# Delta-rule attention in front of a mixture of experts: chunks of 32 tokens in four partition quadrants instead of 64 in two halves, with the TensorE order written out

## The chip, the core and the metric

The kernel runs on one core of a Trainium2 chip. The metric is the device time of one execution in microseconds (us). A second view is one profiled execution, whose trace gives every instruction's start and duration on five engines: TensorE (PE for matmuls, PEld for the weight loads that precede them), VectorE (DVE), ScalarE (ACT), GpSimd (POOL) and SyncE (SP, which here only issues DMAs).

## What is computed

Two stages. The first is a delta-rule recurrence over 768 tokens for each of 4 batches and 8 heads, with head dimension 48; its result, 3072 rows of 384, is the input of a mixture of 16 experts (4 groups of 4), of which each row uses one.

```python
B, H, S, D = 4, 8, 768, 48
k_n = k / (norm(k) + 1e-6)
state = zeros(B, H, D, D)
for t in range(S):
    y[:, :, t] = q[:, :, t] @ state
    v_old = state^T k_n[t]
    state += beta[t] * outer(k_n[t], v[t] - v_old)
x = y as (3072, 384)                      # rows are tokens, heads side by side
g = argmax(x @ w_group);  e = argmax(x @ w_expert[g])
out = weight(g) * weight(e) * (relu(x @ w1[g, e]) @ w2[g, e])      # 384 -> 1024 -> 384
```

Everything is fp32.

## The kernel before

**Chunks.** A recurrence over single tokens would be 768 serial steps. The kernel works on chunks of `C = 64` tokens instead. Inside a chunk the corrected values are `w = M f`, where `f` are the values less what the state already holds for these keys, and `M` is the inverse of a unit lower triangular 64x64 matrix built from the products of the keys. One unit `u` is a chunk of two batches: its 128 tokens fill the 128 partitions, batch one in partitions 0 to 63, batch two in 64 to 127 (`halves`). There are `NU = 24` units: 12 chunks times `NG = 2` pairs of batches.

**`prepare(u)`** does what needs no state. GpSimd scales keys and values (`kp` L190, `vh` L193). TensorE transposes the keys (`kt_ps` L198), ScalarE copies them to `kqt` (L200). For each parity of the head number (`hh`) the products keys-by-keys and keys-by-queries go to `g_ps` (L209), VectorE masks them into `gq` and `mm` (L213, L218), and three GpSimd operations form the start of the inverse (L222 to L225). Then the inverse is doubled level by level: with `LEVELS = (2, 4, 8, 16, 32)` there are five levels, and at each, for each `hh`, 8 matmuls of 64x64 give `y_ps` (L239), VectorE masks them into `y` (L242), 16 matmuls (8 at the last level) give `m_ps` (L249, L251), and ScalarE copies them to the next `mm` (L261, at the last level `mt`, L256). A level can't begin before the copy of the level below it is there.

**`advance(u)`** carries the state `s_bd`: `a_ps` (L273, keys by state), `f` (L278), `w_ps` (L284), `w` (L287), the state's increment `d_ps` (L292) added by VectorE (L299), and `outputs(u)`: `o_ps` (L308, L314), copied to `x` (L318).

**`route(c)`** takes the finished rows of one chunk of all four batches: transposes (`t_ps`, L350), logits (`l_ps`, L355), a chain of some thirty short VectorE, ScalarE and GpSimd operations that picks group and expert and counts the rows per expert (`r_ps`, L389 and L391), the store of the rows to `x_dram` (four DMAs on SP, L380), and one matmul group that adds the rows' places to a table (`p_ps`, L423).

**Order.** The main loop over 12 chunks calls `advance` on the two units of the chunk and `prepare` on those of the next one; the framework's scheduler then decides the order in which each engine runs the instructions, TensorE included. Tiles come from pools with a fixed number of buffers; an instruction that writes a tile waits until the tile's former user is done.

**The experts.** After the last chunk the table is turned into indices (L444 to L453), and 16 experts run with two tiles of 128 rows each: gather by indirect DMA (L461), transposes (L473), two matmul layers (L481, L488), scatter (L492). The weights of the first two experts are loaded during the attention, the others while the experts run.

A fp32 matmul is two passes in the trace: a weight load and a matmul for each of two passes. So the page counts 3840 matmuls on L239 where the program has 24 x 2 x 5 x 8 = 1920. "Pass" below means one such pair.

Of the kernel before, what the change touches and what calls it, by code (L numbers as in the profile page):

```python
# [15 lines left out]
C = 64  # L16
LEVELS = (2, 4, 8, 16, 32)
XW = 388


def constants(n_tokens, seq, n_experts, n_group, n_pairs):
    """Masks and counters that depend on the shapes alone, by name."""
# [4 lines left out]
    twice = lambda m: np.concatenate([m, m], axis=0)  # L27
# [6 lines left out]
        "upper": twice(np.concatenate([upper, upper], axis=1)),  # L34
        "eye": twice(eye),
        "low0": twice(-below(1).astype(np.float32)),
        "up0": twice(eye - below(1).T),
        "level": twice(np.concatenate([eye - below(s) for s in LEVELS], axis=1)),
# [3 lines left out]
        "desc": np.tile(np.arange(n_group, 0, -1), (128, n_pairs)),  # L42
# [10 lines left out]
def deltanet_then_moe(  # L53
# [17 lines left out]
    NG = B // 2  # L71
    NCH = S // C
    NU = NCH * NG
# [9 lines left out]
    STATIC = -(-N // (NE * 128))  # L83
    halves = [slice(0, 64), slice(64, 128)]

# [27 lines left out]
    with ExitStack() as first:  # L113
# [5 lines left out]

        k_all = ap_.tile([128, NU, H, D], F32, name="k_all")  # L120
        bt = ap_.tile([128, NU, H], F32, name="bt")
        ssq = ap_.tile([128, NU, H], F32, name="ssq")
        rs = ap_.tile([128, NU, H], F32, name="rs")
        sb = ap_.tile([128, NU, H], F32, name="sb")
        s_bd = ap_.tile([128, B, NP, 2, D], F32, name="s_bd")
        NB = 4
# [3 lines left out]
        def load_k(u):  # L130
            nc.scalar.dma_start(out=k_all[:, u].rearrange("p h d -> p (h d)"), in_=k_d[u])

        def load_qv(u):
            v = io.tile([128, H, D], F32, tag="v", name=f"v{u}")
            nc.sync.dma_start(out=v.rearrange("p h d -> p (h d)"), in_=v_d[u])
            kqt = kqt_[u % NB]
            for hh in range(2):
                nc.sync.dma_start(out=kqt[hh * 64:hh * 64 + D, 1].rearrange("p j t -> p (j t)"),
                                  in_=q_d[u, hh])
            return v  # L140
# [4 lines left out]
        for u in range(NG):  # L145
            load_k(u)
        nc.scalar.dma_start(out=bt.rearrange("p u h -> p (u h)"), in_=beta_d)
        nc.sync.dma_start(out=con, in_=const_d)
        vs = {u: load_qv(u) for u in range(NG)}
        for u in range(NG, NU):  # L150
            load_k(u)
# [4 lines left out]
        zrow = ap_.tile([1, XW], F32, name="zrow")  # L156
# [3 lines left out]
        def root(out_, in_, shape_, name):  # L160
            """sqrt of in_, with a Newton step in fp32 behind the table; gives twice the root."""
            r0 = sm.tile(shape_, F32, tag=name + "0", name=name + "0")
            r1 = sm.tile(shape_, F32, tag=name + "1", name=name + "1")
# [6 lines left out]
        root(sb, bt, [128, NU, H], "rb")  # L170
# [12 lines left out]

        norms(0, NG, nc.vector)

        def prepare(u):
            """Everything of a chunk that does not need the state: keys and values scaled, the
            products of keys and queries, the inverse of the unit lower triangular matrix."""
            v, kqt, kp = vs.pop(u), kqt_[u % NB], kp_[u % NB]
            nc.gpsimd.tensor_tensor(kp[:, :, 0:D], k_all[:, u],  # L190
                                    rs[:, u, :, None].to_broadcast([128, H, D]), op=ALU.mult)
            vh = wk.tile([128, H, D], F32, tag="vh", name=f"vh{u}", bufs=4)
            nc.gpsimd.tensor_tensor(vh, v, sb[:, u, :, None].to_broadcast([128, H, D]),  # L193
                                    op=ALU.mult)
            kt_ps = ps.tile([128, NP, 128], F32, tag="g", name=f"kt_ps{u}")
# [5 lines left out]

            gqs, mts = [], []
            for hh in range(2):
                g_ps = ps.tile([128, NP, 2, C], F32, tag="g", name=f"g_ps{u}_{hh}")
                rows = slice(hh * 64, hh * 64 + D)
                for j in range(NP):
                    for b in range(2):
                        t = slice(b * C, (b + 1) * C)
                        nc.tensor.matmul(g_ps[halves[b], j], lhsT=kqt[rows, 0, j, t],  # L209
                                         rhs=kqt[rows, :, j, t], start=True, stop=True,  # L210
                                         skip_group_check=True)
                gq = wk.tile([128, NP, 2, C], F32, tag=f"gq{hh}", name=f"gq{u}_{hh}", bufs=3)
                nc.vector.tensor_tensor(  # L213
                    gq.rearrange("p j a t -> p j (a t)"),
                    g_ps.rearrange("p j a t -> p j (a t)"),
                    cut["upper"][:, None, :].to_broadcast([128, NP, 2 * C]), op=ALU.mult)
                mm = wk.tile([128, 2, NP, C], F32, tag=f"mm{hh}", name=f"mm{u}_{hh}_0", bufs=3)
                nc.vector.tensor_tensor(  # L218
                    mm[:, 0], g_ps[:, :, 0, :],
                    cut["low0"][:, None, :].to_broadcast([128, NP, C]), op=ALU.mult)  # L220
                eye = cut["eye"][:, None, :].to_broadcast([128, NP, C])
                nc.gpsimd.tensor_tensor(mm[:, 0], mm[:, 0], eye, op=ALU.add)  # L222
                at = wk.tile([128, NP, C], F32, tag=f"at{hh}", name=f"at{u}_{hh}")
                nc.gpsimd.tensor_tensor(at, gq[:, :, 0, :], eye, op=ALU.add)  # L224
                nc.gpsimd.tensor_tensor(  # L225
                    mm[:, 1], at, cut["up0"][:, None, :].to_broadcast([128, NP, C]),
                    op=ALU.mult)
                gqs.append(gq)
                mts.append((at, mm))

            for n in range(len(LEVELS)):
                last = n == len(LEVELS) - 1
                mask = cut["level"][:, n * C:(n + 1) * C]
                for hh in range(2):
                    at, mm = mts[hh]
                    y_ps = ps.tile([128, NP, C], F32, tag="y", name=f"y_ps{u}_{hh}_{n}")
                    for j in range(NP):
                        for b in halves:
                            nc.tensor.matmul(y_ps[b, j], lhsT=at[b, j], rhs=mm[b, 0, j],  # L239
                                             start=True, stop=True, skip_group_check=True)  # L240
                    y = wk.tile([128, NP, C], F32, tag=f"y{hh}", name=f"y{u}_{hh}_{n}")
                    nc.vector.tensor_tensor(y, y_ps,  # L242
                                            mask[:, None, :].to_broadcast([128, NP, C]),
                                            op=ALU.mult)
                    m_ps = ps.tile([128, 2, NP, C], F32, tag="m", name=f"m_ps{u}_{hh}_{n}")
                    for j in range(NP):
                        for b in halves:
                            if not last:
                                nc.tensor.matmul(m_ps[b, 0, j], lhsT=mm[b, 1, j], rhs=y[b, j],  # L249
                                                 start=True, stop=True, skip_group_check=True)  # L250
                            nc.tensor.matmul(m_ps[b, 1, j], lhsT=y[b, j], rhs=mm[b, 1, j],  # L251
                                             start=True, stop=True, skip_group_check=True)
                    if last:
                        new = wk.tile([128, NP, C], F32, tag=f"mt{hh}", name=f"mt{u}_{hh}",
                                      bufs=3)
                        nc.scalar.activation(new, m_ps[:, 1], ACT.Copy)  # L256
                        mts[hh] = new
                    else:
                        new = wk.tile([128, 2, NP, C], F32, tag=f"mm{hh}",
                                      name=f"mm{u}_{hh}_{n + 1}", bufs=3)  # L260
                        nc.scalar.activation(new, m_ps, ACT.Copy)  # L261
                        mts[hh] = (at, new)
            return kqt, kp, vh, gqs, mts

        def advance(u, made):
            """The chunk's outputs, and the state behind it."""
            c, g = u // NG, u % NG
            kqt, kp, vh, gqs, mts = made
            if c > 0:
                a_ps = ps.tile([128, H, D], F32, tag="q", name=f"a_ps{u}")  # L270
                for b in range(2):
                    for j in range(NP):
                        nc.tensor.matmul(a_ps[halves[b], 2 * j:2 * j + 2, :],  # L273
                                         lhsT=kqt[:, 0, j, halves[b]],
# [152 lines left out]
        for c in range(NCH):  # L427
            nxt = range((c + 1) * NG, min((c + 2) * NG, NU))
            for u in nxt:
                vs[u] = load_qv(u)  # L430
# [147 lines left out]
```

## Time and profile before

| what | value |
|---|---|
| time, median of 3 runs | 1143.3 us (1142.66 to 1143.77) |
| span of the profiled execution | 1145.2 us |
| PE busy / PEld busy | 1026.7 us (90%) / 863.4 us (75%) |
| DVE / ACT / POOL busy | 316.1 / 226.8 / 245.5 us |
| passes on TensorE | 16298 |
| first matmul of the attention (L198) | 34.8 us into the span |
| end of the last logits of the attention (L355) | 761.4 us |
| first transpose of the experts (L473) | 776.4 us |

The profiled execution has a span of 1145.2 us, 1.9 us above the median of the timed runs. The table's lower half splits it: 34.8 us of loading and norms without a matmul, some 726 us of attention, 15 us of the last routing, and 369 us of experts. A matmul's row in the trace shows its whole way through the array (218 ns for a pass of 64 columns); several are under way at once, so "busy" says that something is under way and not how dense it is. How dense it is, the starts in the timeline tell. "PEclk" is the share of TensorE's clock that was granted.

### The profile page before, as it was taken

How to read it: one execution, taken by the hardware profiler on the slowest of the kernel's cores; microseconds unless marked ns; L12 is line 12 of the kernel's file. 1: busy time of each engine (PE TensorE's matmuls, PEld its weight loads, DVE VectorE, ACT ScalarE, POOL GpSimd, SP SyncE). 2: the span in 40 equal slices, each digit the busy share in tenths (PEclk: the TensorE clock that was granted, in tenths of full speed). 3: DMA queues.
4: the chain of work that ended last, by engine and by line, in shares of the span. 5: the costliest groups of instructions: out<-in, count | busy, mean ns of one | idle time of the engine just before them, and what ended most of it. 6: DMA issues, size and time to landing. Idle time of an engine off the chain costs nothing. (4 is left out here: it accounts for less than half of the span.)

```text
span 1145.2 us, 35577 instructions
## 1 busy us (share of the span) xinstructions
PE 1026.7 (90%) x16298; PEld 863.4 (75%) x16298; DVE 316.1 (28%) x983; ACT 226.8 (20%) x429; POOL 245.5 (21%) x389
## 2 busy tenths in 40 slices
PE   0698999999999999998999999978999999999996
PEld 0587888888888887888888888866776677677674
DVE  4533434242423334242334242330100100110010
ACT  0132322222222222222222222210110011011000
POOL 5613122222222222122122221102211211221110
PEclk9999899999999999999999999988999999999998
DMA  9500100000100001010100000003545555464520
GB/s 297 209 11 10 31 17 23 23 24 17 30 17 21 26 17 30 10 30 17 31 9 17 16 17 2 17 16 107 190 146 191 165 185 173 165 199 141 192 68 11
DMA packets 41545, 83.49 MB, mean 73 GB/s; under 512 B 4377, under 2 KB 30156, under 8 KB 41394
## 3 DMA queue, kind: packets, MB, share of 16 engines
q1 hardware_dynamic: 33698, 65.30, 17.8%
q0 software_dynamic: 4096, 11.08, 2.9%
q10 hardware_dynamic: 3600, 4.82, 1.3%
q8 instruction: 128, 2.10, 0.8%
q14 instruction: 23, 0.19, 0.0%
HBM read 71.70 MB, written 11.06 MB: 72 GB/s over the span
## 5 line engine op out<-in xcount | busy, mean ns | idle before, releaser
L239 PE MATMUL y_ps<-mm,at 64*64 64x64 f32 x3840 | 227.7, 229 | 47.0 <-POOL mm L222 41.5
L251 PE MATMUL m_ps<-mm,y 64*64 64x64 f32 x3840 | 248.5, 228 | 0.2
L239 PEld LDWEIGHTS y_ps<-mm,at 64*64 64x64 f32 x3840 | 183.4, 140 | 69.3 <-POOL mm L222 51.9
L251 PEld LDWEIGHTS m_ps<-mm,y 64*64 64x64 f32 x3840 | 223.2, 143 | 2.4 <-DVE y L242 1.2
L249 PE MATMUL m_ps<-y,mm 64*64 64x64 f32 x3072 | 216.2, 233 | 1.3
L249 PEld LDWEIGHTS m_ps<-y,mm 64*64 64x64 f32 x3072 | 195.3, 142 | 16.0 <-DVE y L242 15.2
L242 DVE TENSOR_TENSOR y<-y_ps,con 128x256 f32<-128x256 f32 x240 | 101.8, 424 | 371.7 <-PE y_ps L239 368.7
L261 ACT ACTIVATE mm<-m_ps 128x512 f32<-128x512 f32 x192 | 114.7, 597 | 385.8 <-PE m_ps L251 385.8
L481 PE MATMUL h_ps<-xt,w 128*128 128x256 f32 x768 | 171.6, 384 | 8.1 <-DVE xt L475 8.1
L481 PEld LDWEIGHTS h_ps<-xt,w 128*128 128x128 f32 x768 | 145.9, 192 | 31.2 <-DVE xt L475 11.7
L488 PE MATMUL y_ps<-w,hid 128*128 128x384 f32 x512 | 167.7, 486 | 0.0
L488 PEld LDWEIGHTS y_ps<-w,hid 128*128 128x128 f32 x512 | 97.3, 190 | 64.4
L491 DVE TENSOR_SCALAR yo<-y_ps,xg 128x384 f32<-128x384 f32 x32 | 19.8, 618 | 321.0 <-PE y_ps L488 316.5
L484 ACT ACTIVATE hid<-h_ps 128x512 f32<-128x512 f32 x64 | 38.2, 597 | 322.3 <-PE h_ps L481 322.3
L492 POOL DMA_INDIRECT out_dram<-yo,idx x32 | 32.4, 1012 | 289.9 <-DVE yo L491 285.8
L190 POOL TENSOR_TENSOR kp<-k_all,rs 128x384 f32<-128x384 f32 x24 | 19.8, 829 | 303.9 <-PE g_ps L209 185.8
L209 PE MATMUL g_ps<-kqt 48*64 48x128 f32 x768 | 58.9, 284 | 0.7 <-ACT kqt L200 0.7
L224 POOL TENSOR_TENSOR at<-gq,con 128x256 f32<-128x256 f32 x48 | 34.9, 726 | 77.4 <-DVE gq L213 77.4
L198 PE MATMUL kt_ps<-con,kp 128*128 128x128 f32 x96 | 17.1, 300 | 36.4 <-POOL kp L190 34.8
L209 PEld LDWEIGHTS g_ps<-kqt 48*64 48x64 f32 x768 | 43.0, 137 | 2.3 <-ACT kqt L200 1.1
L284 PE MATMUL w_ps<-f,mt 64*64 64x48 f32 x704 | 43.0, 241 | 0.2 <-DVE f L278 0.2
L273 PE MATMUL a_ps<-s_bd,kqt 128*64 128x96 f32 x352 | 42.4, 262 | 0.0
(115 smaller groups left out, 922.2 us busy)
## 6 DMA issues: line engine op xcount, KB each, us to landing
w<-in_w_dram SPq DMA_DIRECT2D x32, 1536.0 KB, 6.8
x_dram<-x SPq DMA_DIRECT2D x48, 97.0 KB, 2.2
k_all<-in_k_dram ACTq DMA_DIRECT2D x24, 192.0 KB, 4.7
v<-in_v_dram SPq DMA_DIRECT2D x24, 192.0 KB, 2.5
kqt<-in_q_dram SPq DMA_DIRECT2D x48, 96.0 KB, 2.2
con<-in_const_dram SPq DMA_DIRECT2D x1, 708.5 KB, 5.2
xg<-x_dram,idx POOLq DMA_INDIRECT x32, 3.2
out_dram<-yo,idx POOLq DMA_INDIRECT x32, 3.3
```

Source lines behind the costliest of these rows:

```text
L209: nc.tensor.matmul(g_ps[halves[b], j], lhsT=kqt[rows, 0, j, t], rhs=kqt[rows, :, j, t], start=True, stop=True, skip_group_check=True)
L224: nc.gpsimd.tensor_tensor(at, gq[:, :, 0, :], eye, op=ALU.add)
L239: nc.tensor.matmul(y_ps[b, j], lhsT=at[b, j], rhs=mm[b, 0, j], start=True, stop=True, skip_group_check=True)
L242: nc.vector.tensor_tensor(y, y_ps, mask[:, None, :].to_broadcast([128, NP, C]), op=ALU.mult)
L249: nc.tensor.matmul(m_ps[b, 0, j], lhsT=mm[b, 1, j], rhs=y[b, j], start=True, stop=True, skip_group_check=True)
L251: nc.tensor.matmul(m_ps[b, 1, j], lhsT=y[b, j], rhs=mm[b, 1, j], start=True, stop=True, skip_group_check=True)
L261: nc.scalar.activation(new, m_ps, ACT.Copy)
L273: nc.tensor.matmul(a_ps[halves[b], 2 * j:2 * j + 2, :], lhsT=kqt[:, 0, j, halves[b]], rhs=s_bd[:, 2 * g + b, j], start=True, stop=True, sk ...
L284: nc.tensor.matmul(w_ps[b, h], lhsT=mts[h % 2][b, h // 2], rhs=f[b, h], start=True, stop=True, skip_group_check=True)
L481: nc.tensor.matmul(h_ps[:, k], lhsT=w1[:, j, (f + k) * 128:(f + k + 1) * 128], rhs=xt[:, j], start=(j == 0), stop=(j == DC - 1), skip_grou ...
L484: nc.scalar.activation(hid[:, f:f + 2], h_ps, ACT.Relu)
L488: nc.tensor.matmul(y_ps, lhsT=hid[:, f, i * 128:(i + 1) * 128], rhs=w2[:, f], start=(f == 0), stop=(f == FC - 1))
```

## The change

The chunk shrinks to `C = 32`, and a unit is now the same 32 tokens of all four batches, one batch in each quadrant of 32 partitions (`quads`). There are 24 units again, but they are now 24 serial steps of the state instead of 12 steps of two. The inverse needs four levels instead of five. Its matmuls are 32x32: for each level 32 for `y_ps` and 64 for `m_ps` (32 at the last), each on the quadrant of the array that its batch's partitions give. Both parities of the head number share one tile and one VectorE or ScalarE operation.

`prepare`, `advance`, `logits` (split from `route`) and `route` become generators that hand over after each stage, and a loop of `period`s of four `tick`s steps them: three chunks are in `prepare` at once, the oldest first, `advance` is three periods behind, `logits` four, and `route` runs once for every `RG = 4` chunks. Inside `tc.manual_schedule` TensorE runs in exactly this order; the other engines' order is still the scheduler's. Most PSUM tiles share one pool of four banks (tag `s`); `g_ps` and the two `d_ps` share two tiles of two banks. The rows' store is 16 DMAs of 32 rows for each `route`, where it was 4 of 64 for each chunk.

```diff
-C = 64
-LEVELS = (2, 4, 8, 16, 32)
+C = 32
+LEVELS = (2, 4, 8, 16)
+RG = 4
...
     halves = [slice(0, 64), slice(64, 128)]
+    quads = [slice(b * C, (b + 1) * C) for b in range(B)]
...
+        def prepare(u):
...
+            kt_ps = ps.tile([128, NP, 128], F32, tag="s", name=f"kt_ps{u}", bufs=4)
...
+            yield
+            g_ps = ps.tile([128, 2, 512], F32, tag="g", name=f"g_ps{u}")
...
+            for j in range(NP):
+                for b in range(B):
+                    for hh in range(2):
+                        rows = slice(hh * 64, hh * 64 + D)
+                        nc.tensor.matmul(g_out[quads[b], hh, j], lhsT=kqt[rows, 0, j, quads[b]],
+                                         rhs=kqt[rows, :, j, quads[b]], start=True, stop=True,
...
+            yield
+            yield
+            yield
+            for n in range(len(LEVELS)):
+                last = n == len(LEVELS) - 1
+                y_ps = ps.tile([128, H, C], F32, tag="s", name=f"y_ps{u}_{n}", bufs=4)
+                for h in range(H):
+                    for b in quads:
+                        nc.tensor.matmul(y_ps[b, h], lhsT=at[b, h], rhs=mm[b, 0, h],
+                                         start=True, stop=True, skip_group_check=True)
+                y = wk.tile([128, H, C], F32, tag="y", name=f"y{u}_{n}", bufs=4)
+                nc.vector.tensor_tensor(y, y_ps, wide(cut["level"][:, n * C:(n + 1) * C]),
+                                        op=ALU.mult)
+                yield
+                m_ps = ps.tile([128, 2, H, C], F32, tag="s", name=f"m_ps{u}_{n}", bufs=4)
+                for h in range(H):
+                    if not last:
+                        for b in quads:
+                            nc.tensor.matmul(m_ps[b, 0, h], lhsT=mm[b, 1, h], rhs=y[b, h],
+                                             start=True, stop=True, skip_group_check=True)
+                    for b in quads:
+                        nc.tensor.matmul(m_ps[b, 1, h], lhsT=y[b, h], rhs=mm[b, 1, h],
+                                         start=True, stop=True, skip_group_check=True)
...
+                yield
+
+        def advance(u):
...
+                for j in range(NP):
+                    for b in range(B):
+                        nc.tensor.matmul(a_ps[quads[b], 2 * j:2 * j + 2, :],
+                                         lhsT=kqt[:, 0, j, quads[b]], rhs=s_bd[:, b, j],
...
+            yield
...
+            yield
...
+                        for b in range(B):
+                            hh = (b + odd) % 2
+                            nc.tensor.matmul(d_out[odd][halves[hh], b // 2, j],
+                                             lhsT=kp[quads[b], 2 * j + hh],
...
+            yield
+            yield
...
+        with tc.manual_schedule(engines={mybir.EngineType.PE}):
+            for period in range(NCH + 7):
+                u = period
+                for tick in range(4):
...
+                    if tick == 2:
+                        if u == 0:
+                            norms(2, 6, nc.gpsimd)
+                        if u == 1:
+                            norms(6, NCH, nc.gpsimd)
+                        if u + 1 < NCH:
+                            scale(u + 1)
+                    for v in (u - 2, u - 1, u):
+                        step("prepare", v)
+                    step("advance", u - 3)
+                    if tick % 2:
+                        step("logits", u - 4)
+                    step("route", (u - 5) // RG)
```

Read along the ticks, TensorE's order within one full period is: `y` of level 2 of the oldest chunk and of level 0 of the middle one (levels counted from 0), `kt` of the youngest, `a`; then `m` of those two levels, `g`, `w`, the state's part of `o`, and the transposes `t` of the chunk before; then `y` of levels 3 and 1, `d`, the rest of `o`; then `m` of levels 3 and 1, the logits `l`, and every fourth period the routing's `r` and `p`.

## The prediction, made before the changed kernel ran

> **What bounds the kernel now.** First the stretches of the span, cut at the first matmul, the last logits and the first transpose of the experts. Columns: length, then busy us and instructions of each engine, the granted clock, DMA.
>
> ```profile
> 0.00:34.80 34.80, 0.00 (x0) 0.00 (x0) 16.30 (x35) 1.75 (x3) 22.28 (x41) 1.00 0.93 317
> 34.80:760.50 725.70, 671.90 (x14902) 603.82 (x14902) 258.04 (x843) 186.38 (x360) 158.45 (x279) 0.95 0.08 23
> 760.50:776.40 15.90, 6.05 (x20) 4.45 (x20) 6.88 (x41) 0.46 (x3) 3.88 (x9) 0.57 0.17 41
> 776.40:1145.20 368.80, 348.70 (x1376) 255.11 (x1376) 34.92 (x64) 38.23 (x64) 60.92 (x62) 0.98 0.45 149
> ```
>
> The change touches the first 776 us; 368.8 us of experts stay. In the attention TensorE has something under way 93% of the time, and no other engine is above 36%. It needs 725.7 / 14902 = 48.7 ns a pass. What a pass costs when nothing waits, the timeline shows within one level of the inverse:
>
> ```profile
> 303.18 0.33 PE L249 MATMUL m_ps<-y,mm 64*64 64x64 f32 x4
> 303.29 0.33 PE L251 MATMUL m_ps<-mm,y 64*64 64x64 f32 x4
> 303.41 0.33 PE L249 MATMUL m_ps<-y,mm 64*64 64x64 f32 x4
> 303.52 0.33 PE L251 MATMUL m_ps<-mm,y 64*64 64x64 f32 x4
> 303.64 0.33 PE L249 MATMUL m_ps<-y,mm 64*64 64x64 f32 x4
> ```
>
> Four passes start every 0.117 us, 29.3 ns each. Two batches work in two tiles of the array, so one tile takes 58.6 ns a pass. The other 19 ns of the 48.7 are waits, changes of tile shape, longer matmuls, and a clock of 0.95. The waits for the copies are visible in the waits' view as PEld m_ps L249 behind DVE (15.2 us) and y_ps L239 behind POOL (48.7 us).
>
> Now the price of a change of tile shape, and of a round trip through ScalarE:
>
> ```profile
> 757.47 0.33 PE L308 MATMUL o_ps<-s_bd,kqt 128*64 128x96 f32 x2
> 757.73 1.01 PEld L314 LDWEIGHTS o_ps<-w,gq 64*64 64x64 f32 x32
> 757.73 1.13 PE L314 MATMUL o_ps<-w,gq 64*64 64x48 f32 x32
> 758.80 0.84 PE L355 MATMUL l_ps<-wr,xt 128*128 128x20 f32 x6
> 758.91 0.49 ACT L318 ACTIVATE x<-o_ps 128x384 f32<-128x384 f32 x1 [1.76 <-PE o_ps L314]
> 759.49 0.52 PE L350 MATMUL t_ps<-con,x 128*128 128x128 f32 x3
> ```
>
> From the last pass of one shape to the first of the next it is 0.16 to 0.17 us (757.56 to 757.73; the o burst's last start, 758.80 less 0.16, to 758.80). A pass of 48 columns (32 in 1.13 us, less the last one's 0.22: 29.4 ns) costs what one of 64 does, so the load of 64 weight columns sets it. l_ps, 128 weight columns and 20 moving ones, takes (0.84 - 0.275) / 5 = 113 ns. The round trip: o ends at 758.86, ScalarE's copy ends at 759.40, the transpose that needs it starts at 759.49: 0.6 us.
>
> **The change: passes.** The program now has 24832 passes in the attention instead of 14902, because each inverse is cut finer: 4 x 32 + 3 x 64 + 32 = 352 matmuls, 704 passes a chunk, against 448 for a unit before. All depends on what a 32x32 pass costs, which the trace does not have. By the two load rows (58.6 ns at 64 columns, 113 at 128: 0.85 ns a column and 4 ns fixed) one tile would take 31 ns. Four quadrants at once make that 7.9 ns a pass. The other end is 29.3 ns, if what I see is a rate of issue and not of the tiles. The nearest row for more than two tiles is a place where y and d interleave:
>
> ```profile
> 92.87 0.22 PE L239 MATMUL y_ps<-mm,at 64*64 64x64 f32 x1
> 92.87 0.26 PE L292 MATMUL d_ps<-w,kp 64*64 64x48 f32 x3
> 92.93 0.22 PE L239 MATMUL y_ps<-mm,at 64*64 64x64 f32 x1
> 92.97 0.23 PE L292 MATMUL d_ps<-w,kp 64*64 64x48 f32 x2
> 92.99 0.22 PE L239 MATMUL y_ps<-mm,at 64*64 64x64 f32 x1
> 93.03 0.23 PE L292 MATMUL d_ps<-w,kp 64*64 64x48 f32 x2
> ```
>
> Ten passes start in 0.16 us, some 17 ns each: 29 ns is no rate of issue, at least in a short burst. A second bound is the fetch of instructions:
>
> ```profile
> q8 instruction: 128, 2.10, 0.8%
> ```
>
> 128 packets took 0.8% of 16 engines x 1145 us, 1.15 us each; they brought 2 x 16298 instructions, 255 a packet, so one packet serves 128 passes: 9.0 ns a pass if the packets follow each other without a gap. I take 9.0, the tile's 7.9 raised to the fetch.
>
> [...]
>
> **One full period**, in us of TensorE:
> - y, m: 704 x 9.0 = 6.3; g: 64 x 9.0 = 0.6
> - w and o: 128 passes of 48 moving columns. L488 of the experts moves 384 columns in 323 ns, 0.84 ns a column, so 44 ns a tile, 11 with four: 1.4
> - a and the state's part of o: 64 passes of 96 columns. Before, one batch after the other, a_ps takes 94 ns a pass ((0.92 - 0.26) / 7 at 301.81); the new loop alternates four tiles, 23.5: 1.5
> - d: 64 passes that load 64 columns, four row tiles, 58.6 / 4 = 14.7: 0.9
> - 7 transposes at 0.124 (kt at 328.39: (0.66 - 0.29) / 3): 0.9; logits 6 x 0.113 = 0.7; p and r, a quarter of 8 x 0.32 + 4 x 0.12: 0.8
> - 12 changes of shape (y-kt-a-m-g-w-o-t-y-d-o-l-y) at 0.17: 2.0
>
> Sum 15.1. **Waits.** The order puts other bursts between each burst and its copy: after y2, y0, kt and a (2.4 us) cover DVE's 0.42 us and the way; m's copies (ACT, 0.60 for 128x512) are covered by g, w, o, t; the state additions (four of 64x384; 0.36 at 64x192, 0.55 at 128x384, taken 0.55: 2.2 us) by o, m3, m1, l, y, kt, 5 us. If that cover is gone, each place costs 0.6 or more. One place has none: in the pool of four banks m3's tile is the one that o leaves, so m3 waits for x (L318): 0.6 us. Queues: DVE gets 5.8 us a period from its rows (0.69 + 0.42 + 4 x 0.42 + 0.55 + 2.2 + 0.2) and 2 of routing, ACT 4.3, POOL 3.9 and 1, all below 15. In each fourth period some 30 routing operations of 0.16 to 0.21 us stand in DVE's order between y's masks, and one of them waits for POOL; m waits behind that. I take 3 us, 0.75 a period; bounds 0 and 8 (all of them in the way). Period: 15.1 + 0.6 + 0.75 = 16.5 us.
>
> **The ends.** The first matmul stays at 34.8: its chain (24 loads on ACT's queue before the root) is the same. POOL then has 13 operations of 0.82 us before the first inverse's start where it had five, so y0 comes at 48 instead of 43; two unfilled periods, bound by round trips, 9 to 10 us each: the first full period begins at 67. 21 full periods follow (chunks 3 to 23 in `prepare`), then four that empty: 14.5, 12, 6, 2.2 = 35 us. The last routing took 15 us up to the experts' first transpose; now 16 stores of the rows stand on SP instead of 4 (0.58 us each in L380's rows, 9.3 us) and the gather waits for all: +4. In full flow SP's stores delay the loads of later queries, which have a whole period. Experts 368.8.
>
> Sum: 67 + 21 x 16.5 + 35 + 19 + 369 = 836 us against a span of 1145.2. The median of the runs is 1.9 us below that span; I leave it out.
>
> **Rivals.**
> 1. Slower: passes start at a fixed rate whatever their size, 29 ns, and the 17 ns was only a filled queue. For: no burst of one line before runs below 26 ns a pass. Against: starts come in pairs 4 ns apart and then nothing for 54, the picture of two busy tiles. Price: y, m, g 768 x 20 ns, w and o 128 x 18, d 64 x 15, a 64 x 6: +19 us, a period of 35.5, 1236 us. It decides from (1145 - 490) / 21 = 31.2 us a period, about 25 ns a pass.
> 2. Two quadrants at a time, or instructions fetched with gaps: 16 ns a pass, +6 us a period, 965.
> 3. The written order covers less than I think: a round trip bare in each tick with its queue, 4 x 1 us: 920.
> 4. The clock. It falls to 0.5 for 3.4 us after gaps; if passes this small count as idle, every matmul doubles: 31 us a period, about 1150, no change.
>
> That the change does nothing is excluded: order and number of passes differ in the build.
>
> **Chances.** Forecast (785 to 900) 58%; 2 and 3 (900 to 1040) 27%; 1 is 8%, 4 is 4%, both at 1100 and above; below 785 (DVE-free, 7.9 ns) 3%. Range 785 to 1040. Runs of one kernel here lie within 0.1%, so 0.2% is what can be told from no change: faster 0.88, same 0.02, slower 0.10.
>
> **What would show it.** In a new m burst, 16 passes in 0.14 us; if 0.26, rival 2; if 0.47, rival 1. From the first transpose of one chunk to that of the next 16.5 us, with no PE gap above 0.7 us but before m3 and in routing periods. PEclk at 1.0 throughout. q8's packets back to back would show the fetch at its limit. I am wrong if TensorE's passes are dense and yet the period is above 20.

## The result: 1161.3 us, 1.5% slower

| kernel | time, median | ratio to the kernel before | mean clock |
|---|---|---|---|
| before | 1143.1 us (1142.66 to 1143.77) | 1 | 0.955 |
| after | 1161.3 us (1160.06 to 1161.71, 4 runs) | 1.0151 [1.0129, 1.0173] | 0.772 |

The forecast of 836 us was far off, and the change went the other way. Ratios here and below stand with their 95% interval, each against runs of the kernel before that were taken beside it. "Mean clock" is the granted share of TensorE's clock over the profiled execution. The profiled execution of after has a span of 1159.9 us.

**Where the time went.** The stretches of after, cut next to the first matmul (30.9 us), the end of the last logits (771.3) and the first transpose of the experts (790.7). Columns as in the prediction's first view: length, then busy us and instructions of PE, PEld, DVE, ACT and POOL, the granted clock, DMA.

```profile
0.00:30.90 30.90, 0.04 (x1) 0.04 (x1) 14.88 (x38) 1.87 (x4) 20.62 (x44) 1.00 0.99 316
30.90:772.00 741.10, 516.69 (x24820) 442.65 (x24820) 174.89 (x493) 105.58 (x204) 110.33 (x211) 0.66 0.09 25
772.00:791.00 19.00, 7.14 (x16) 4.41 (x17) 7.89 (x42) 0.43 (x2) 5.75 (x16) 0.59 0.24 60
791.00:1159.90 368.90, 349.02 (x1376) 255.19 (x1374) 34.90 (x64) 38.23 (x64) 60.56 (x61) 0.98 0.44 149
```

The start, the routing's end and the experts are as forecast. The attention takes 741 us for 24820 passes, 29.9 ns a pass, where 9 had been assumed. TensorE has something under way for only 70% of it, no other engine for more than a quarter. So TensorE is idle and waits, but for what? The groups of TensorE give the releaser in the last column:

```profile
L257 PE MATMUL m_ps<-mm,y 32*32 32x32 f32 x6144 | 144.5, 218 | 65.0 <-issue 65.0
L254 PE MATMUL m_ps<-y,mm 32*32 32x32 f32 x4608 | 122.4, 218 | 59.9 <-issue 59.0 <-DVE y L247 0.9
L218 PE MATMUL g_ps<-kqt 48*32 48x64 f32 x1536 | 29.5, 283 | 18.8 <-issue 18.1 <-ACT kqt L210 0.7
```

"issue" is idle time in which the engine waited for nothing that the profile shows: no semaphore, no tile, no data. Before, that column named mostly DVE, ACT and POOL, and little stood in it for the same products:

```profile
L251 PE MATMUL m_ps<-mm,y 64*64 64x64 f32 x3840 | 248.5, 228 | 0.2
L239 PE MATMUL y_ps<-mm,at 64*64 64x64 f32 x3840 | 227.7, 229 | 47.0 <-POOL mm L222 41.5 <-ACT mm L261 3.5
```

Now the timeline of after, in the middle of an m burst and of the g burst after it:

```profile
414.73 0.31 PE L257 MATMUL m_ps<-mm,y 32*32 32x32 f32 x8
414.83 0.31 PE L254 MATMUL m_ps<-y,mm 32*32 32x32 f32 x8
...
416.85 0.23 PE L257 MATMUL m_ps<-mm,y 32*32 32x32 f32 x4
418.48 0.18 PE L257 MATMUL m_ps<-mm,y 32*32 32x32 f32 x1 [1.41 <-issue]
...
418.57 0.25 PE L257 MATMUL m_ps<-mm,y 32*32 32x32 f32 x8
418.64 0.25 PE L254 MATMUL m_ps<-y,mm 32*32 32x32 f32 x8
418.70 0.25 PE L257 MATMUL m_ps<-mm,y 32*32 32x32 f32 x8
...
419.17 0.96 PE L218 MATMUL g_ps<-kqt 48*32 48x64 f32 x62
422.07 0.42 PE L218 MATMUL g_ps<-kqt 48*32 48x64 f32 x2 [1.93 <-issue]
```

Two things. While passes start, they are as dense as forecast: 24 passes from 418.57 on start at 8 per 0.065 us, 8 ns each, and 13 ns at half clock (8 per 0.105 us at 414.73). But a burst breaks off in the middle, with one operand pattern and no dependence between its neighbours, for 1.4 to 2 us.

The breaks fall into step with the instruction packets. This is the DMA view of after for 405 to 425 us; the row "GB/s" has 40 slices of 0.5 us, and each 33 that stands alone is one 16 KB packet:

```profile
GB/s 0 33 0 0 0 0 0 0 33 0 0 0 0 0 0 33 0 0 0 0 0 0 33 0 95 267 31 0 0 33 0 0 0 0 0 0 33 0 0 0
q8 instruction: 6, 0.10, 1.9%
```

A packet every seven slices, 3.5 us, although each keeps the queue for only about 1 us and the DMA engines do next to nothing else. The page has 206 of them in the whole execution, 1.2% of the engines' time:

```profile
PEclk9856576666676766666666666767999999999998
q8 instruction: 206, 3.38, 1.2%
```

From the packets' start times in the trace: between 70 and 740 us they are a median 3.59 us apart (10% 3.39, 75% 3.77). Before they were never closer than 4.2 us (median 5.6). Gaps over 0.5 us between the starts of TensorE's instructions add up to 261 us between 60 and 760 us, before to 52. Of the gaps of after, 142 between 70 and 760 us (236 us) end 0.9 to 1.8 us after the end of a packet, and 135 of these 142 stand at one and the same place in a block of 256 TensorE instructions. One round can be read off there, in medians: 1.14 us from the end of a stall to the start of the next packet, 0.99 us for the packet, 1.38 us from its end to the first instruction that runs again. The sum is 3.51 us, close to the median distance of 3.59. A packet holds 256 instructions, 128 passes: 3.59 / 128 = 28 ns a pass.

The 256 agree with the trace: 52545 records of TensorE, 52420 of them matmuls and weight loads, in 206 packets, 255 each. The fetch is not hidden behind the work here: TensorE uses up 128 passes in 1.0 to 1.7 us (8 to 13 ns each), and the next block comes 3.59 us after the one before in the median.

### The profile page after: what moved, and what is told of

It reads as the page before. It is cut to its first block, busy times and chain, and to the rows that moved or that the text cites. A ratio compares the mean times of both kernels' runs of the same rounds, so it can differ in the third digit from the quotient of the medians.

```text
span 1159.9 us, 54681 instructions
## 1 busy us (share of the span) xinstructions
PE 872.9 (75%) x26210; PEld 702.3 (61%) x26210; DVE 232.6 (20%) x635; ACT 146.1 (13%) x274; POOL 197.3 (17%) x331
## 5 line engine op out<-in xcount | busy, mean ns | idle before, releaser
L257 PE MATMUL m_ps<-mm,y 32*32 32x32 f32 x6144 | 144.5, 218 | 65.0 <-issue 65.0
L257 PEld LDWEIGHTS m_ps<-mm,y 32*32 32x32 f32 x6144 | 131.5, 131 | 71.4 <-issue 71.3
L254 PE MATMUL m_ps<-y,mm 32*32 32x32 f32 x4608 | 122.4, 218 | 59.9 <-issue 59.0
L254 PEld LDWEIGHTS m_ps<-y,mm 32*32 32x32 f32 x4608 | 110.0, 130 | 68.5 <-issue 65.5
L244 PE MATMUL y_ps<-mm,at 32*32 32x32 f32 x6144 | 90.9, 224 | 24.7 <-issue 12.9
L244 PEld LDWEIGHTS y_ps<-mm,at 32*32 32x32 f32 x6144 | 82.1, 137 | 38.6 <-issue 24.6
L265 ACT ACTIVATE mm<-m_ps 128x512 f32<-128x512 f32 x72 | 43.0, 597 | 231.4 <-PE m_ps L257 228.0
L247 DVE TENSOR_TENSOR y<-y_ps,con 128x256 f32<-128x256 f32 x96 | 40.6, 423 | 137.2 <-PE y_ps L244 135.6
L321 DVE TENSOR_TENSOR s_bd<-d_ps,s_bd 64x384 f32<-64x384 f32 x92 | 51.0, 555 | 18.7 <-PE d_ps L308 16.7
L286 PE MATMUL w_ps<-f,mt 32*32 32x48 f32 x1472 | 36.9, 270 | 18.5 <-issue 17.8
L208 PE MATMUL kt_ps<-con,kp 128*128 128x128 f32 x96 | 24.9, 410 | 32.5 <-POOL kp L193 30.9
```

What stands on the lines that cost most here:

```text
L208: nc.tensor.transpose(out=kt_ps[:, j], in_=kpf[:, j * 128:(j + 1) * 128], identity=ident)
L244: nc.tensor.matmul(y_ps[b, h], lhsT=at[b, h], rhs=mm[b, 0, h], start=True, stop=True, skip_group_check=True)
L247: nc.vector.tensor_tensor(y, y_ps, wide(cut["level"][:, n * C:(n + 1) * C]), op=ALU.mult)
L254: nc.tensor.matmul(m_ps[b, 0, h], lhsT=mm[b, 1, h], rhs=y[b, h], start=True, stop=True, skip_group_check=True)
L257: nc.tensor.matmul(m_ps[b, 1, h], lhsT=y[b, h], rhs=mm[b, 1, h], start=True, stop=True, skip_group_check=True)
L265: nc.scalar.activation(mm, m_ps, ACT.Copy)
```

## The experiments

Three theories were kept apart. **Theory 1**, supply: TensorE gets 128 passes for each 3.5 us. **Theory 2**, a fixed rate of issue: passes start no closer than some 25 to 29 ns (rival 1 of the prediction). **Theory 3**, the array itself, slow at the half clock that PEclk shows.

### Passes alone, without data to wait for

```python
with tc.manual_schedule(engines={mybir.EngineType.PE}):
    for n in range(256):                       # qa, qb (16 columns), qd: the four quadrants
        for b in quads:
            mmul(qa[b, 0:32], lhsT=a[b, n % 16, 0:32], rhs=a[b, n % 16, 32:64], ...)
    for n in range(256):                       # hc: two halves, the kernel before's form
        for b in halves:
            mmul(hc[b, 0:64], lhsT=a[b, n % 16, 0:64], rhs=a[b, n % 16, 64:128], ...)
    # one: a single quadrant; he: 64x64 on four tiles; full: 128x128
    # a 4.7 MB store of zeros and an 8 MB load on SP's queue
```

The kernel computes nothing of the reference; it only issues streams of matmuls on constant operands. The load is written ahead of qd, but it has nothing to wait for and ran at the start, beside qa.

> Streams of matmuls without any wait, in place of the whole kernel: qa and qd 1024 matmuls of 32x32 over four quadrants (qa beside a load of 8 MB), qb the same with 16 moving columns, hc 512 of 64x64 over two halves, one 512 of 32x32 in a single quadrant, he 512 of 64x64 over all four tiles, full 128 of 128x128. Theory 1 (supply: TensorE's instructions come in packets of 256, 128 passes, one packet at a time, one in some 3.5 us): qd, qb and he all at 27 ns a pass on the mean, in bursts of 128 passes at 8 ns (qd, qb) or 15 (he) with a gap of 1.5 to 2.5 us behind each; hc 29 and one 31, bound by the tile, without gaps; full 113. Theory 2 (a fixed rate of issue): qd, qb, he evenly spaced at 25 to 29 ns, no gaps. Theory 3 (the clock): qd at 8 ns, or 13 while the clock is at half, no gaps.

Time 331.0 us. Mean from start to start, between the first and the last pass of each stream:

| stream | ns a pass | in bursts | gaps over 0.4 us |
|---|---|---|---|
| qa, four quadrants 32x32, beside the load and the store | 34.6 | 13.3 | 15, 43.8 us |
| qb, the same, 16 columns moved | 28.3 | 13.3 | 16, 30.9 us |
| qd, as qa | 26.6 | 12.5 | 15, 29.1 us |
| he, four 64x64 tiles | 27.3 | 17.1 | 6, 10.5 us |
| hc, two 64x64 tiles | 31.2 | 31.2 | none |
| one, one quadrant | 51.2 | 51.2 | none |
| full, 128x128 | 112.1 | 112.1 | none |

The groups of this kernel, idle time behind the second bar:

```profile
L45 PE MATMUL one<-a 32*32 32x32 f32 x1024 | 52.6, 232 | 0.0
L41 PE MATMUL hc<-a 64*64 64x64 f32 x1024 | 32.2, 226 | 0.0
L36 PE MATMUL qb<-a 32*32 32x16 f32 x2048 | 30.6, 209 | 27.6 <-issue 27.6
L62 PE MATMUL qd<-a 32*32 32x32 f32 x2048 | 29.1, 229 | 25.6 <-issue 25.6
L51 PE MATMUL he<-a 64*64 64x64 f32 x1024 | 18.9, 237 | 9.2 <-issue 9.2
```

The clock of he, from the view of stretches (length, busy us and instructions of PE, PEld, DVE and POOL, granted clock, DMA):

```profile
216.60:244.60 28.00, 18.80 (x1027) 17.95 (x1024) 0.00 (x0) 0.00 (x0) 0.90 0.02 4
```

Every stream whose passes could start closer than 27 ns has idle time labelled "issue" and comes out at 26.6 to 28.3 in the mean (34.6 beside the load); every stream that needs longer has none. Moving half the columns (qb) buys nothing. All 52 stalls over 0.5 us in these streams are at the same place in a block of 256 as in after. Theory 2 falls: it would space the passes evenly, and here they come at 12.5 to 17 ns and then stop. Theory 3 falls too: it has no gaps, and he comes out at 27.3 ns with a granted clock of 0.90. The expectation missed one number: the stream in one quadrant was to take 31 ns a pass and took 51.2, without gaps, because it ran mostly at a granted 0.50 (the last section has its rows). So 25 to 29 ns is not a distance that the passes keep; 27 to 28 is what they are given in the mean.

### Wider passes, the same number of them

```diff
-nc.tensor.matmul(y_ps[b, h], lhsT=at[b, h], rhs=mm[b, 0, h], ...)
+nc.tensor.matmul(y_ps[b, h], lhsT=at[b, h], rhs=mmf[b, h * C:(h + 2) * C], ...)
```

The 32 further columns of each pass are computed and not used.

> The changed kernel with y_ps matmuls of 64 moving columns instead of 32 (the second 32 columns are never read): same passes, more work in 256 of the 1040 passes of a period. Theory 1: no change, 1161 us within 6, the longer passes fill the gaps. Theory 2: no change either. Theory 3 (or any theory in which the tiles' own time counts): 256 x 7 ns more a period at full clock, 256 x 13 at half, 40 to 75 us slower.

1175.7 us (1172.0 to 1180.1), 1.0274 [1.0237, 1.0311] of before, 14 us over after. Outside theory 1's 6 us, and far below the 40 to 75 of theory 3. The groups of this kernel, the same y line that had 90.9 us busy and 24.7 idle in after:

```profile
L245 PE MATMUL y_ps<-mm,at 32*32 32x64 f32 x6144 | 146.7, 271 | 18.3 <-POOL mm L234 9.4 <-issue 6.6 <-ACT mm L267 2.2
```

56 us more under way in 6144 passes, and a quarter of that in time. The gaps over 0.5 us shrink from 261 to 249 us, and the packets come 3.72 us apart in the median instead of 3.59. Why the time is not the same stays open.

### Fewer passes

```diff
-                    if not last:
-                        for b in quads:
-                            nc.tensor.matmul(m_ps[b, 0, h], lhsT=mm[b, 1, h], rhs=y[b, h], ...)
...
-                    nc.scalar.activation(mm, m_ps, ACT.Copy)
+                    nc.scalar.activation(mm, m_ps[:, 1:2].to_broadcast([128, 2, H, C]), ACT.Copy)
```

This leaves out the first product of each level (4608 passes), so that the inverse is not formed; all else keeps its place.

> The changed kernel without the first of the two products of each level (L254); the next level takes the other product twice, so the inverse is not the reference's. 4608 of 24832 passes less, every wait stays. Theory 1: 36 packets less at 3.5 us, 126 us less, 1035. Theory 2: 4608 x 25 to 29 ns, 115 to 134 less. Theory 3: 4608 x 8 to 13 ns, 37 to 60 less, 1100 to 1125.

1033.1 us in one run, 128.2 below after: 128200 / 4608 = 27.8 ns for each pass that is gone, though such a pass occupies 8 to 13 ns of a burst. That is the distance of the packets over 128, a second time, and outside theory 3's 37 to 60 us. The page has 170 packets instead of 206.

### The 32x32 matmuls undone: batches in pairs

```diff
-    i, k = np.meshgrid(np.arange(C), np.arange(C), indexing="ij")
+    i, k = np.meshgrid(np.arange(2 * C), np.arange(2 * C), indexing="ij")
...
-    upper = (i < k).astype(np.float32)
+    upper = ((i < k) & (i // C == k // C)).astype(np.float32)
...
-                y_ps = ps.tile([128, H, C], F32, tag="s", name=f"y_ps{u}_{n}", bufs=4)
+                y_ps = ps.tile([128, H, 2 * C], F32, tag="s", name=f"y_ps{u}_{n}", bufs=4)
...
-                    for b in quads:
+                    for b in halves:
```

Two batches share a 64x64 matmul, one on each diagonal block; the masks clear the blocks between. Chunks of 32, four batches a unit, three chunks in flight and the written order stay. The attention has 14080 passes instead of 24832. (m_ps moves to the larger tiles of tag "g", and some buffers are fewer to make room.)

> The changed kernel (chunks of 32, three in flight, the written order) with the batches taken in pairs again: two 32x32 blocks on the diagonal of one 64x64 matmul, the blocks off the diagonal masked to zero, so g, y, m, w and o need half the matmuls. 14080 passes in the attention instead of 24832. Theory 1: 110 packets x 3.5 us = 385 us is no longer the bound; the tiles are: 352 x 29.3 + 32 x 56 (g) + 64 x 29 (w, o) + 6 for the rest and the changes of shape, some 20 to 23 us a period, 930 to 1000 us. Theory 2: 14080 x 29 = 408 us and the changes of shape, about the same. Theory 3: the clock at 1.0 again, about the same. If the period of the changed kernel is bound by the order's waits and not by the passes, it stays near 29 us and the time near 1150.

**928.9 us (928.0 to 930.4), 0.8121 [0.8103, 0.8138] of before.** The same product is formed with redundant zeros, and it is 232 us faster than after and 214 faster than before. Its attention in the view of stretches, and its rows of clock and packets:

```profile
32.00:538.20 506.20, 467.81 (x14068) 430.90 (x14068) 229.36 (x518) 141.36 (x204) 155.31 (x217) 0.98 0.12 35
...
PEclk9989999999999999999999978999999999999998
q8 instruction: 122, 2.00, 0.9%
```

TensorE is under way 92% of the stretch, at a granted clock of 0.98. A period is 18.8 us (26 with routing). Packets are 4.0 us apart in the median: the 31 ns a pass that two 64x64 tiles need (hc above) are just slower than the supply.

### The written order left to the scheduler

```diff
-        with tc.manual_schedule(engines={mybir.EngineType.PE}):
+        if True:
```

> The changed kernel with one part undone: TensorE's order is not written out but chosen by the framework's scheduler, as in the kernel before; the 32x32 matmuls and their number stay. Theory 1 (instructions reach TensorE at one packet for about 3.6 us, 27 ns a pass): the order hardly matters, since the same 24832 passes must be fetched; 1161 us to 1230, the upper end if waits for copies now fall where the fetch cannot run ahead of them. Rival, the order is what counts and the fetch fills gaps that are there anyway: the scheduler's order costs what separates the kernel before (48.7 ns a pass) from the paired kernel (36 ns a pass), 12 ns x 24832 = some +300 us; above 1400.

1157.6 us (1156.3 to 1161.4), ratio 1.0119 [1.0088, 1.0151], which overlaps with that of after. The stalls add up to 262 us, and the packets are 3.53 us apart. But the order of TensorE is not another one. Tile by tile, the 26210 matmuls of the two traces stand in the same sequence but for 6 places where two bursts meet: the scheduler kept the order in which the loop of periods and ticks writes the program. So this run undoes the fixing of the order and not the order. The same edit on the paired kernel:

> The paired kernel without the written TensorE order (the framework's scheduler orders TensorE, as in the kernel before and in the run called loose). It closes a square of four: 32x32 or paired 64x64 matmuls, with and without the written order. Theory (with 32x32 matmuls the order was worth nothing because instructions came too slowly; with pairs the order can count, since 14080 passes need only 14080 x 27.8 ns = 391 us of fetch in an attention of 506): if the gain of the paired kernel over the one before lies in the written order, 1000 to 1150 us; if it lies in the 32-token chunk, the four batches a unit and three chunks in flight, whoever orders them, 915 to 960 us. By the run loose I expect the second, since the scheduler there gave the same time as the written order, but there nothing else could show.

929.4 us (928.9 to 931.7), 0.8133 [0.8114, 0.8151]; the paired kernel with the order written out had 0.8121. Here too the sequence is the same, but for 20 of 15458 matmuls, all where the routing's `p` meets `y`. So fixing the order with `manual_schedule` is worth nothing measurable in either kernel; what the order itself is worth no run here shows, and the rival of the expectations that the order counts was not tested. The runs split the change in two: all that surrounds the matmuls (32-token chunks with four levels, four batches to a unit, three chunks in flight, in the order of the loop) brings 214 us, and cutting the matmuls to 32x32 takes 232 back. How the 214 us divide among those parts is not shown.

### Two terms of the prediction by themselves

The prediction priced a routing period by VectorE's queue. In the paired kernel, where supply doesn't hide it, this moves eight operations of it to GpSimd:

```diff
-                nc.vector.tensor_scalar(col, cut["iota"][:, 0:128], at[:, g, 0:1], None,
+                nc.gpsimd.tensor_scalar(col, cut["iota"][:, 0:128], at[:, g, 0:1], None,
...
-                nc.vector.tensor_scalar(row, cut["iota"], ex[:, g], idv[:, g],
+                nc.gpsimd.tensor_scalar(row, cut["iota"], ex[:, g], idv[:, g],
```

> The paired kernel with the eight operations that build col and row of the routing (L436, L439) on GpSimd instead of VectorE. In the paired kernel every fourth period, the one with routing, takes 26.0 us instead of 18.8, with 2.7 us in which TensorE waits behind VectorE (y and s_bd stand behind the routing's operations) and then some 3.4 us at half clock. If VectorE's queue is the price of a routing period, as the prediction's step says: 2 to 5 us less in each of 6 periods, 900 to 917 us. Rival, the matmuls that need row then wait for GpSimd, which takes longer for each: no gain, 925 to 940.

937.6 us (937.0 to 939.3), 0.8197 [0.8177, 0.8217], 8.7 us slower than the pairs. The rival holds, as this line of its waits says:

```profile
PEld p_ps L447 <- POOL row L439: 30.7, 14, 4.6
```

One row takes 1645 ns on GpSimd and 473 on VectorE; the wait moved to p_ps. The attention ends 5.1 us later and the last routing takes 4.1 us more.

The term for a and o took 94 ns for a pass of 96 columns on one tile, shared by as many tiles as alternate. Tried in the kernel before:

```diff
-                for b in range(2):
-                    for j in range(NP):
+                for j in range(NP):
+                    for b in range(2):
```

> The kernel before with two loops turned inside out: in a_ps and in the state's part of o_ps the two batches now alternate, so that neighbouring passes go to different halves of the array (704 passes of 96 columns, 94 ns each in the trace of before). Nothing else changes. Theory: one tile takes 94 ns for such a pass and two tiles overlap, as the prediction's term for a and o assumes (94 / 4 with four tiles): 47 ns, 704 x 47 = 33 us less if none of it was covered, 1111 to 1128 us. Rival, these bursts lie beside waits that then show: within 5 us of 1143.

1138.1 us (1133.3 to 1145.8), 0.9955 [0.9926, 0.9984]. The price per pass was right: a_ps went from a mean of 97 ns to 49, the state's part of o_ps from 90 to 56. The time followed by only 5 us of the 33 (2 to 8 by the interval): two units take 61 us on average (58.6 to 62.9) where they took 61.4. The clock is a candidate for the rest: the attention of this trace was granted 0.91, that of before 0.95, which over 725 us is up to 29 us of full-clock time (an estimate from these two rows), and of its ten runs the four at 0.925 and 0.926 took 1143 to 1146 us, the six at 0.936 to 0.943 1133 to 1139. Whether the lower clock or a wait took the gain was not separated.

## Why the prediction was wrong

**The step that failed** is the second bound on the price of a pass: "one packet serves 128 passes: 9.0 ns a pass if the packets follow each other without a gap". 1.15 us is about the time that a packet takes (a mean of 1.09 us in the trace of before, 1.07 in that of after); the distance of two in after is 3.25 us at the least and 3.59 in the median. The term should have been 28 ns, and the condition "if ... without a gap" was written down and then not examined. The trace of before could have shown it: there packets never started closer than 4.2 us, 33 ns a pass. Its DMA view for 300 to 320 us (40 slices of 0.5 us) has them in the tenth, nineteenth and thirty-second slice, 4.7 and 6.3 us apart:

```profile
GB/s 0 0 0 0 0 0 0 0 0 33 68 264 52 9 0 0 0 0 33 16 174 9 133 143 134 183 3 0 0 0 0 33 0 0 0 0 0 0 0 0
q8 instruction: 3, 0.05, 1.1%
```

That was an upper end, since TensorE's own 48.7 ns a pass make 6.2 us for the 128 of a packet, but no row showed packets 1.15 us apart. With 28 ns for each of the 24832 passes the attention takes 695 us and the whole about 1115 (30.9 + 695 + 20 + 369, an estimate from after's own rows). That forecast would have stood 2% below the kernel before instead of 27%; the rest up to 1161 is put down, without a run of its own, to the thin ends, where passes wait for round trips, and to routing periods.

**Rival 2** named the cause in half a clause ("instructions fetched with gaps") and priced it at 16 ns, again from no row. **Rival 1** (1236 us) and **rival 4** (about 1150) came near the time by luck, with causes that the streams rule out.

**Point by point.**
- The tile's price, 7.9 ns with four quadrants: right, 8 ns in the bursts at full clock. So were the prices of a and o (23.5 taken; in the pairs' timeline 32 passes of a_ps in 0.87 us less the last one's 0.25, 20) and of d (14.7 taken, 64 in 1.04 less 0.22, 13).
- The full period, 16.5 us taken: 20 periods from 79.8 to 687.9 us, 30.4 each, four to seven us more in those with routing. The 13.9 us that a period was taken too short make 292 of the 324 us that the sum missed, over 21 periods.
- "First full period begins at 67": 79.8. Of these 12.8 us the supply is not the cause, or not all of it: the pairs come there at 79.2. Their unfilled periods took 14.9, 17.8 and 14.4 us, where the sum had 9 to 10 us for two of them, bound by round trips. That term was too small, although the first `y` came at 43.2 us and not at the 48 taken.
- The drain, 35 us taken: from 687.9 to the end of the last logits at 771.3 are 83 us, one full period and 53 more; the pairs, which are starved little, need 38 there. So the term was about right, and the supply is the likely rest.
- The last routing, 19 taken: 771.3 to the first transpose at 790.7, 19.4. Experts 368.8 taken, 369.3.
- The routing's 3 us in each fourth period, taken from VectorE's queue: in the pairs such a period is 7.2 us longer, of which p and r are some 3.7 us of matmuls, the rest a wait of 2.7 us behind VectorE and its aftermath. This is the wait in the pairs' timeline:

```profile
186.42 1.15 PE L257 MATMUL m_ps<-mm,y 64*64 64x64 f32 x32 [2.70 <-DVE s_bd L321]
```

  Right in size there; that VectorE's queue sets it rests on this releaser alone, since taking eight operations off that queue made the kernel slower. In after the longer routing periods were not split into their parts.
- "PEclk at 1.0 throughout": wrong, 0.66 in the attention. The half clock doesn't set the price of a pass: he stalls at a granted 0.90, and drop_m0 gives 27.8 ns for a pass that occupies 8 to 13.
- "q8's packets back to back would show the fetch at its limit": they are at their limit, but with 2.5 us between one's end and the next one's start. "I am wrong if TensorE's passes are dense and yet the period is above 20" looked for the wrong sign: they are dense in bursts and absent between them. The sign "16 passes in 0.14 us" was met in the bursts (8 per 0.065 us at full clock) while the forecast failed, so it couldn't tell.

## What to carry to other kernels

Price a stream of small matmuls twice, by what the array takes and by what the instruction queue delivers, and take the distance between the packets in the trace for the second, not their duration. In these runs 128 passes came per 3.5 us, 27 to 28 ns a pass: where passes could start closer than that, smaller matmuls saved nothing and more of them cost in full, and fewer and larger ones, half filled with zeros, won. Idle time labelled "issue" on an engine that waits for nothing, recurring every 256 instructions, was the sign. And before a run counts as a test of an order, compare the order in its trace.

## What the runs showed of the hardware that was not expected

- Instructions reach TensorE in blocks of 256 (255 records to a packet in after), one at a time (0.99 us each in the median, never less than 3.25 us from start to start): in stalls the next packet starts 1.14 us after the block before it came into use, and its instructions run 1.38 us after it has landed. What passes in these two stretches the trace does not show.
- Beside the load and the store (174 GB/s during qa) the packets of qa came up to 7 us apart, and 3.4 again after the load; its mean of 34.6 ns is the highest of the quadrant streams.
- A stream in one quadrant without a gap (one) fell to half clock: 14.3 us at a granted 0.62 (3.4 us at 0.99, where a pass takes 32 ns, then 0.50), then 0.50 to its end, where a pass takes 53.3 ns, while two 64x64 tiles (0.93) and 128x128 (1.00) kept it up. These are the stretches of the streams' profile, the two halves of one, hc before them:

```profile
132.00:164.10 32.10, 32.10 (x1032) 32.04 (x1024) 0.00 (x0) 0.00 (x0) 0.93 0.02 5
164.10:178.40 14.30, 14.30 (x313) 14.28 (x310) 0.00 (x0) 0.00 (x0) 0.62 0.01 2
178.40:216.50 38.10, 38.10 (x719) 38.10 (x716) 0.00 (x0) 0.00 (x0) 0.50 0.01 3
```

  TensorE has something under way all the time in each of the three. So the half clock of after need not come from the stalls alone; how much each of the two adds was not separated. A stream of small passes at half clock without a gap is the prediction's rival 4 in kind; by what rule the clock is granted no run shows. In after the half clock was hidden behind the supply.
